# The second product of the last three chunks by Strassen's scheme: linear attention and a squared-ReLU layer on one core

## The chip, the cores and the metric

One core of one Trainium2 chip (trn2). The number that counts is the device time of one launch in microseconds. Before the change three runs took 1060.15, 1060.94 and 1062.51 us; the median is 1060.94.

## What is computed

Eight batches of eight heads, 576 tokens, head size 64. A linear attention gives each token 512 numbers, and a two-layer network follows; everything is float32 in and out.

```
phi(x) = [exp(p), exp(-p)],  p = x @ w_phi - max|x @ w_phi|        # 64 -> 2 x 128
num = phi(q) @ (phi(k).T @ v);  den = phi(q) @ sum(phi(k)) + 1e-6
x   = num / den                                                    # 4608 tokens x 512
out = relu(x @ w_in) ** 2 @ w_out                                  # 512 -> 2048 -> 512
```

## The kernel before, in words

The work comes in two streams that share the engines. The attention goes through 32 pairs of heads (four pairs to a batch): the first six pairs by `early` (L661), the others by `visit` (L842) and `late` (L905). What a pair yields goes into a ring buffer of tokens as two float16 halves (`tokens`, L805), scaled by a power of two that `batch_scale` (L548) finds for each batch from the largest sum of |v|.

The layer takes the 4608 tokens in 18 chunks of 256, and each chunk in 8 blocks of 256 hidden units: 144 blocks, written by `moe(c, f)` (L994), numbered n = 8c + f. A block has a **first product** on TensorE (L1012), 24 matmuls of 256 columns: w_in and x are each held as a high and a low float16 half, and three of the four half products are summed. ScalarE takes the relu out of PSUM (L1021), squares it into `gh` (float32r, L1023) and once more into the PSUM bank (L1025); VectorE subtracts the two into a bfloat16 remainder `gl` (L305, called at L1028). Then the **second product** (L1040), 12 matmuls of 512 columns: low w_out with the upper half of `gh`, high w_out with `gh`, near w_out with `gl`, for two groups of 128 tokens and two groups of 128 hidden units. It adds up over the 8 blocks of a chunk in two PSUM banks `po`, which VectorE scales into `o` (L1058) and SP's queue stores (L1069). The first product has two PSUM buffers `ph`; one comes free when VectorE has made `gl`. `gh` and `gl` have three buffers each.

Once per launch w_in and w_out are read, rounded and split on VectorE, ScalarE and GpSimd (L420 to L540). They go to homes in SBUF that stay until the end: `win`, and `wh` and `wl` for w_out.

The order of all this is fixed when the program is built. Every step is added to a planner (`Plan`, L78) with its engine, what it waits for, the buffers it uses and a rank; `order` (L150) plays the plan through, giving each engine the ready step of least rank, and each engine's instructions are written in that order. Steps with ranks between -50 and `MOVED` (70.0, L51) don't keep the rank of the code: `improve` (L141) takes it from a table of numbers, `RANKS`, 1107 of them.

Of the kernel before, what the change touches and what calls it, by code (L numbers as in the profile page):

```python
# [35 lines left out]
NCH = NT // T  # L36
RING = 6 * T
# [13 lines left out]
MOVED = 70.0  # L51
# [26 lines left out]
class Plan:  # L78
# [71 lines left out]
    def order(self):  # L150
# [20 lines left out]
        def release(op):  # L171
            least = max([open_at.get(tag, 0.0) for tag, n in alone(op)] + [a.start + 0.001 for a in op.behind], default=0.0)
# [74 lines left out]
class Tiles:  # L247
# [44 lines left out]
def tile_kernel(ctx, tc, qp, kp, vp, w_phi, w_in, w_out, out):  # L292
# [64 lines left out]
    vm_ = tiles(sm, "vm", [128, NP], F32, 2)  # L357
# [12 lines left out]
    o_ = tiles(mp, "o", [128, DM], F32, 2)  # L370

# [176 lines left out]
    def batch_scale(b, rank):  # L548
        last = []
        for i in range(NP):  # L550
# [3 lines left out]
                accum_out=vm_[b][:, i:i + 1]), [v_load[p]], [("v", p), ("vm", b), ("sx", ("va", p))], rank))  # L554
        d = cb[:, b, :]

        o = power(lambda: m1[b], d, TOP_X, [P.add("DVE", 0.2, lambda: V.tensor_reduce(
            out=m1[b], in_=vm_[b], op=ALU.max, axis=AX.X), last, [("vm", b)], rank)], [], rank)
        t0, t1 = b * S, (b + 1) * S
# [13 lines left out]
        scale_of[b] = P.add("DVE", 0.33, tokens, [o], [], rank)  # L573
# [234 lines left out]
    def tokens(p, nums, rank):  # L808
# [11 lines left out]
        for c0, c1 in cuts:  # L820
# [8 lines left out]
            def high(to=to, c0=c0, c1=c1):  # L829
                A.activation(out=to(0), in_=rb_[p][:, c0:c1], func=AF.Copy, scale=cb[:, b, 1:2])  # L830

            def low(to=to, c0=c0, c1=c1):
                V.scalar_tensor_tensor(out=to(1), in0=rb_[p][:, c0:c1], scalar=cb[:, b, 1:2], in1=to(0),
# [4 lines left out]
                    out=to(0), in0=rb_[p][:, c0:c1], scalar1=cb[:, b, 1:2], scalar2=None, op0=ALU.mult), 4.0))  # L838
# [155 lines left out]
    def moe(c, f, w_done):  # L994
# [9 lines left out]

        def gemm1():
# [11 lines left out]
        if f:  # L1017
            g1.after.append(chunk_done[c][-1])
        chunk_done.setdefault(c, []).append(g1)
        Q = m - 1000.0  # L1020
        o = P.add("ACT", act_us(512, 1), lambda: A.activation(  # L1021
# [6 lines left out]
        o = P.add("DVE", 0.70, lambda: sub(V, gl_[n], ph_[bank], gh_[n].bitcast(F32)),  # L1028
                  [o, sq], [("ph", bank), ("gh", n), ("gl", n)], Q)


        def gemm2():
# [5 lines left out]
            for s, i, j in turns:  # L1038
                g, w = ((gh_[n], highs[f]), (upper(gh_[n]), low), (gl_[n], near))[s]
                PE.matmul(out=po_[po[i][1]], lhsT=g[:, j, 128 * i:128 * i + 128], rhs=w[:, j, :],  # L1040
                          start=(f == 0 and (s, j) == (1, 0)), stop=(f == NFP - 1 and (s, j) == (2, 1)))

        g2 = P.add("PE", 2.74, gemm2, [o] + list(w_done[f, False]),
                   [("gh", n), ("gl", n)] + po, m + 1.5)
        if f:
            g2.after.append(last2[0])
        last2[0] = g2
        if f == NFP - 1:
# [3 lines left out]
    def store(c, i, po, g2, Q):  # L1052
        tt = 2 * c + i

        def scaled(E, x):
            to, of, k = o_[tt][:, x], po_[po[1]][:, x], cc[:, tt:tt + 1]
            if E is V:
                V.tensor_scalar(out=to, in0=of, scalar1=k, scalar2=k, op0=ALU.mult, op1=ALU.mult)  # L1058
            else:
                A.activation(out=to, in_=of, func=AF.Copy, scale=cc2[:, i:i + 1])  # L1060

        ways = ((V, slice(0, DM)),)
        if c == NCH - 1:
            ways = (V, slice(0, DM // 2)), (A, slice(DM // 2, DM))
        for E, x in ways:
            n = x.stop - x.start
            o = P.add(*(("DVE", dve_us(n) + 0.11) if E is V else ("ACT", out_us(n) + 0.09)), lambda E=E, x=x: scaled(E, x),
                      [g2] + [scales] * (E is A), [po, ("o", tt)], Q)
            P.add("SP", 0.38, lambda x=x: SP.dma_start(out[128 * tt:128 * tt + 128, x], o_[tt][:, x]), [o], [("o", tt)], Q,  # L1069
                  land=1.8, xfer=0.7)  # L1070
# [9 lines left out]
    def make_ring1():  # L1080
        stage.close()
        whole = ctx.enter_context(tc.tile_pool(name="late", bufs=1, side="right")).tile(
            [128, 2, KT, HR], F16, name="ring1")
# [21 lines left out]
    for p in range(NPAIR):  # L1105
        if p % NP == 0 and p:
# [3 lines left out]
            batch_scale(b, PER_PAIR * p + 1.0)  # L1110
# [3 lines left out]
        if p == EARLY:  # L1114
# [4 lines left out]
    cc2 = sm.tile([128, 2], F32, name="cc2")  # L1119
    last_cc = cc[:, 2 * NCH - 2:2 * NCH]  # L1120
    scales = P.add("DVE", 0.2, lambda: V.tensor_tensor(out=cc2, in0=last_cc, in1=last_cc, op=ALU.mult),
                   [scale_of[B - 1]], [], PER_PAIR * NPAIR, lock=4.0)
    for c in range(NCH):
        for f in range(NFP):
            moe(c, f, w_done)
    pool_next.after += pool_prep
    for op in P.ops:
        op.after = [x for a in op.after for x in (chunk_done[a[1]] if isinstance(a, tuple) else [a])]
# [65 lines left out]
```

## Time and profile before

| | us |
|---|---|
| median of three runs | 1060.94 |
| the profiled execution | 1060.65 |
| its span, first to last instruction | 1058.9 |
| TensorE busy | 1029.8 |
| VectorE busy | 744.2 |
| ScalarE busy | 632.3 |
| GpSimd busy | 135.6 |

The profiled execution is a run of its own: 1.75 us of its time lie outside the span. In the rows PE is TensorE's matmul, PEld its weight load, DVE VectorE, ACT ScalarE, POOL GpSimd, SP the engine that issues the DMAs. A group's row has the line of the code, the engine, the operation, output<-input by the program's names, the shapes, the count, and then busy time in us with the mean of one in ns; behind it stands the engine's idle time ahead of these instructions and what ended it. A matmul's duration includes its way through the array, so steps are read from start to start.

### The profile page before, as it was taken

What the parts mean: (1) busy time and instruction counts of PE and PEld (TensorE: products, weight loads), DVE (VectorE), ACT (ScalarE), POOL (GpSimd) and SP (SyncE); (2) the same over time, 40 slices, a digit from 0 to 9 for tenths busy, and PEclk for the clock granted to TensorE, in tenths of its full rate; (3) what the DMA queues carried; (4) which work ended last, traced back from release to release, by engine and by line L of the source; (5) the groups of instructions that cost most, each with busy time, mean ns of one, the idle gap of its engine ahead of it and who ended that gap; (6) DMA issues with size and microseconds to landing.
All of it is one profiled execution on the core that took longest, in us unless ns stands there. A gap on an engine that the chain in (4) does not pass through costs nothing.

```text
span 1058.9 us, 19521 instructions
## 1 busy us (share of the span) xinstructions
PE 1029.8 (97%) x7762; PEld 713.3 (67%) x7762; DVE 744.2 (70%) x1549; ACT 632.3 (60%) x1130; POOL 135.6 (13%) x66
## 2 busy tenths in 40 slices
PE   7887999999999999999999999999999999999998
PEld 5555666767676676666666667666766767677775
DVE  5899987987977868989878777877686775111111
ACT  5988875656667556755666655666565565333333
POOL 0011223011122001111111111111110111000000
PEclk9999999999999999999999999999999999999999
DMA  9634421221312211212222221112120101000000
GB/s 357 242 122 139 153 75 50 64 71 30 90 52 89 57 54 57 81 53 69 65 57 77 57 67 36 53 56 77 44 65 22 48 9 50 1 21 20 1 21 20
DMA packets 66143, 73.47 MB, mean 69 GB/s; under 512 B 35204, under 2 KB 44036, under 8 KB 64004
## 3 DMA queue, kind: packets, MB, share of 16 engines
q1 hardware_dynamic: 66052, 72.22, 21.8%
q8 instruction: 61, 1.00, 0.4%
q14 instruction: 30, 0.25, 0.1%
HBM read 59.18 MB, written 12.99 MB: 68 GB/s over the span
## 4 chain that ended last, share of the span: by engine, by line
PE 87%; DVE 7%; DMA 4%; ACT 1%; issue 1%; SPq 0%; DVEq 0%; ACTq 0%
PE po L1040 35%; PE ph L1012 34%; PE pv L645 5%; PE pn L863 3%; PE pp L589 2%; PE pv L863 2%; PE pp L933 2%; DMA rd<-rc 1%; PE pn L933 1%; PE pv L650 1%; DMA rb<-rd 1%; PE pn L595 1%; DVE u L466 1%; DVE rb L811 1%; DVE km L605 1%
## 5 line engine op out<-in xcount | busy, mean ns | idle before, releaser
L1012 PE MATMUL ph<-ring,win 128*128 128x256 f16 x3456 | 399.9, 273 | 1.4 <-DVE win L535 0.9
L1012 PEld LDWEIGHTS <-win 128*128 128x128 f16 x3456 | 336.3, 98 | 72.2 <-issue 8.7
L1021 ACT ACTIVATE r<-ph,cw 128x512 f32<-128x512 f32 x144 | 98.8, 686 | 227.1 <-PE ph L1012 226.6
L305 DVE TENSOR_TENSOR gl<-ph,gh 128x512 bf16<-128x512 f32 x144 | 98.5, 684 | 170.4 <-ACT ph L1025 169.0
L946 POOL PARTITION_ALL_REDUCE mx<-pt x52 | 113.6, 2184 | 615.5 <-ACT pt L309 441.6
L1040 PE MATMUL po<-wh,gh 128*128 128x512 f32 x576 | 184.2, 441 | 0.0
L1040 PE MATMUL po<-wl,gh 128*128 128x512 bf16 x576 | 148.6, 380 | 1.5 <-ACT gh L1023 1.4
L1040 PE MATMUL po<-wl,gl 128*128 128x512 bf16 x576 | 149.5, 382 | 0.0
L1040 PEld LDWEIGHTS po<-wh,gh 128*128 128x128 f32 x576 | 108.7, 189 | 33.0
L1023 ACT ACTIVATE gh<-r 128x512 fp32r<-128x512 f32 x144 | 91.0, 632 | 6.1 <-PE po L1040 1.5
L1040 PEld LDWEIGHTS <-gl 128*128 128x128 bf16 x576 | 44.7, 98 | 73.6 <-issue 31.7
L1040 PEld LDWEIGHTS <-gh 128*128 128x128 bf16 x576 | 53.4, 98 | 54.4 <-issue 11.4
L1025 ACT ACTIVATE ph<-r 128x512 f32<-128x512 f32 x144 | 83.9, 583 | 0.0
L645 PE MATMUL pv<-e,v 128*64 128x256 f32 x512 | 64.1, 392 | 3.0 <-ACT kz L309 1.4
L309 ACT ACTIVATE n<-pn 128x320 f32<-128x320 f32 (+1 forms) x32 | 13.8, 430 | 82.0 <-PE pn L863 81.1
L960 DVE SCALAR_TENSOR_TENSOR pt<-qe,zc,pt 128x576 f32<-128x576 f32 x52 | 42.4, 816 | 26.5 <-ACT pt L958 26.0
L305 DVE TENSOR_TENSOR qe<-pt,mx 128x576 f32<-128x576 f32 x52 | 39.1, 753 | 18.0 <-POOL mx L946 17.4
L611 ACT ACTIVATE e<-e 128x512 f32<-128x512 f32 x64 | 39.7, 621 | 19.5 <-DVE e L608 19.3
L645 PEld LDWEIGHTS pv<-e,v 128*64 128x64 f32 x512 | 36.7, 142 | 20.3 <-issue 3.2
L951 ACT ACTIVATE qe<-qe 128x576 f32<-128x576 f32 x52 | 35.0, 673 | 22.4 <-DVE qe L305 22.4
L958 ACT ACTIVATE pt<-qe,zc 128x576 f32<-128x576 f32 x52 | 40.2, 774 | 4.3
L964 DVE STREAM_TRANSPOSE yt<-pt 128x576 f32<-128x576 f32 x52 | 40.4, 776 | 1.5
(203 smaller groups left out, 1265.6 us busy)
## 6 DMA issues: line engine op xcount, KB each, us to landing
v<-in_vp_dram SPq DMA_DIRECT2D x32, 320.0 KB
k<-in_kp_dram SPq DMA_DIRECT2D x32, 288.0 KB
q<-in_qp_dram SPq DMA_DIRECT2D x32, 288.0 KB
rb<-rd SPq DMA_DIRECT2D x64, 144.0 KB
out_dram<-o SPq DMA_DIRECT2D x34, 256.0 KB
td<-kvs SPq DMA_DIRECT2D x26, 128.0 KB
kz<-td SPq DMA_DIRECT2D x104, 32.0 KB
raw3i<-in_w_in_dram SPq DMA_DIRECT2D x1, 1024.0 KB
```

Source lines behind the costliest of these rows:

```text
L305: eng.tensor_tensor(out=out_, in0=a, in1=b_, op=ALU.subtract)
L645: PE.matmul(out=to[64 * h:64 * h + 64, 0:256], lhsT=v_[p][:, t, h, :], rhs=e_[2 * p + h][:, t].rearrange("p s f -> p (s f)"), start=t == 0 ...
L863: PE.matmul(out=to[64 * h:64 * h + 64, :], lhsT=kz_[n][:, 128 * s_ + 64 * h:128 * s_ + 64 * h + 64], rhs=qe_[2 * n + h].rearrange("p (s x) ...
L946: o = P.add("POOL", par_us(S), lambda n=n, h=h: G.partition_all_reduce(mx_[n], pt_[p][:, h, :], channels=128, reduce_op=bass_isa.ReduceOp. ...
L958: o = P.add("ACT", act_us(S, 1), lambda h=h, qe=qe, y=y: A.activation(out=y(), in_=qe(0), func=AF.Copy, scale=zc_[p][:, 2 * h:2 * h + 1]), ...
L960: o = P.add("DVE", dve_us(S), lambda h=h, qe=qe, y=y: V.scalar_tensor_tensor(out=y(), in0=qe(1), scalar=zc_[p][:, 2 * h + 1:2 * h + 2], in ...
L964: o = P.add("DVE", dve_us(S), lambda n=n, y=y: V.transpose(yt_["y", n - 2 * EARLY], y()), [o], [("pt", p), ("yt", ("y", n - 2 * EARLY))], ...
L1012: PE.matmul(out=ph[:, j, :], lhsT=win[w][:, t, 128 * ff:128 * ff + 128], rhs=ring[half][x][:, t, c0:c0 + T], start=k == 0, stop=k == 3 * K ...
L1021: o = P.add("ACT", act_us(512, 1), lambda: A.activation(out=r_[n], in_=ph_[bank], func=AF.Relu, scale=cw[:, f, 0:1]), [g1], [("ph", bank), ...
L1023: sq = P.add("ACT", act_us(512), lambda: A.activation(out=gh_[n], in_=r_[n], func=AF.Square), [o], [("r", n), ("gh", n)], Q)
L1025: o = P.add("ACT", 0.59, lambda: A.activation(out=ph_[bank], in_=r_[n], func=AF.Square), [o], [("ph", bank), ("r", n)], Q, other=("DVE", 0 ...
L1040: PE.matmul(out=po_[po[i][1]], lhsT=g[:, j, 128 * i:128 * i + 128], rhs=w[:, j, :], start=(f == 0 and (s, j) == (1, 0)), stop=(f == NFP - ...
```

## The change

From chunk 15 on (`C0`), but for the very last block of chunk 17, a block's second product is done by Strassen's scheme. The 256 x 256 block of g (two token groups, two hidden groups) and the 256 x 512 block of w_out (two hidden groups, two output halves) are each cut in four; seven sums of the quarters are formed on either side, and seven products take the place of eight. Each is three matmuls of 256 columns in float16 (high with high, high with low, low with high), and each adds up over a chunk in half a PSUM bank of its own, in banks that the attention has left (`bank`). At the end of a chunk `gather` forms the four quarters of the output. This needs the following:

- `split_out`: for each of the 8 hidden blocks w_out is put together again from `wh` and `wl`, three groups of sums are formed, and the seven pieces split into float16 halves `sw`, most of them written over `wh` and `wl` once chunk 14 has read these.
- `norm`, `split_norms`, `tail_scale`: scales that keep the float16 in range, from norms of w_in's columns and of a chunk's tokens (ScalarE square, VectorE reduce, GpSimd all-reduce, a row of tiny VectorE steps).
- `batch_scale`: batches 6 and 7 share one scale, so v of batch 7 is also loaded, ahead of time, into one buffer `j`, and its |v| summed there.
- `RANKS`: 2432 numbers where there were 1107, for all steps with ranks up to 250, the whole program.

The core of the diff:

```
-MOVED = 70.0
+MOVED = 250.0
+C0 = 15
+LASTB = C0 * T // S
...
+    def split_block(c, f, n, ph, g1, m, Q):
...
+        o = P.add("ACT", act_us(512, 1), lambda: A.activation(
+            out=r_[n], in_=ph_[ph], func=AF.Relu, scale=cw_[c][:, f:f + 1]), [g1, norm_x[c]], ...
+        for t in range(2):
+            sq.append(P.add("ACT", act_us(256), lambda t=t: A.activation(
+                out=g()[:, 3 * t:3 * t + 6:5], in_=r_[n][:, :, 128 * t:128 * t + 128], func=AF.Square), ...
+        ss = [P.add("DVE", dve_us(256), ... ALU.add), ...
+              P.add("DVE", dve_us(256), ... ALU.subtract), ...
+              P.add("DVE", dve_us(128), ... ALU.add), ...]
+        o = P.add("ACT", act_us(896), lambda: A.activation(out=gh(), in_=g()[:, 1:8], func=AF.Copy), ss, ...
+        o = P.add("DVE", dve_us(896), lambda: sub(V, gl(), g()[:, 1:8], gh()), [o], ...
...
+        def products(some):
+            for i in some:
...
+                for k, (l, r) in enumerate(((gh, w["hi"]), (gh, w["lo"]), (gl, w["hi"]))):
+                    PE.matmul(out=to, lhsT=l()[:, a], rhs=r(slice(b_, b_ + 1))[:, 0], ...
...
+    def split_out(f, rank):
...
+        def whole():
+            V.tensor_tensor(out=flat_w()..., in0=highs[f]..., in1=wout[f][1]..., op=ALU.add)
...
+        for (at_, n), sm_, src, us_ in zip(WPART, sums, srcs, use):      # 512, 512, 512 and 256 columns
+            o = whole_op
+            if sm_:
+                o = P.add("DVE", dve_us(256 * n), sm_, ...
+            o = P.add("ACT", out_us(256 * n) + 0.09, lambda x=x, src=src: A.activation(
+                out=hi(x), in_=src(), func=AF.Copy, scale=wts[:, 3:4]), ...
+            o = P.add("DVE", dve_us(256 * n), lambda x=x, src=src: V.scalar_tensor_tensor(
+                out=lo(x), in0=src(), scalar=wts[:, 3:4], in1=hi(x), op0=ALU.mult, op1=ALU.subtract), ...
...
+    def gather(c, g2, kx, x_at, ky, y_at, Q):
+        first = [P.add("ACT", out_us(512) + 0.09, lambda j=j: A.activation(
+            out=a()[:, 2 * j:2 * j + 2], in_=x_at(j), func=AF.Copy, scale=ks()), ...) for j in range(2)]
+        o1 = P.add("DVE", dve_us(512), lambda: V.tensor_tensor(... first ...)
+        o = P.add("DVE", dve_us(512), lambda: V.tensor_tensor(... first ...)
+        o = P.add("DVE", dve_us(512), lambda: V.scalar_tensor_tensor(... [o, g2[1]] ...)
+        o2 = P.add("DVE", dve_us(512), lambda: V.scalar_tensor_tensor(... [o, g2[2]] ...)
...
     def store(c, i, po, g2, Q):
...
+        for x in (slice(0, 256), slice(256, 512)):
...
+            o = P.add("DVE", dve_us(256), lambda x=x, to=to: V.scalar_tensor_tensor(
+                out=to(), in0=po_[po[1]][:, x], scalar=cc2[:, 0:1], in1=to(), op0=ALU.mult, op1=ALU.add), ...
```

How the order moves, at three places. **TensorE, inside a second product**, before: the last of the low halves, the four with `wh`, the first with the remainder; po are the output banks, wh and wl parts of w_out.

```order
L1040 LDWEIGHTS gh_11442
L1040 MATMUL po_11429<-wl_642,gh_11442 128x512
L1040 MATMUL po_11426<-wh_631,gh_11442 128x512 x2
L1040 MATMUL po_11429<-wh_631,gh_11442 128x512 x2
L1040 LDWEIGHTS gl_11445
L1040 MATMUL po_11426<-wl_642,gl_11445 128x512
```

And now, one of the seven products (sw holds the split sums of w_out, its high half first, then its low half; v is the buffer in which the remainder lies):

```order
L1315 LDWEIGHTS gh_11035
L1315 MATMUL po_10983<-sw_10663,gh_11035 128x256
L1315 LDWEIGHTS gh_11035
L1315 MATMUL po_10983<-sw_10663,gh_11035 128x256
L1315 LDWEIGHTS v_11040
L1315 MATMUL po_10983<-sw_10663,v_11040 128x256
```

Twelve matmuls of 512 columns have become 21 of 256: seven of these groups of three.

**VectorE where chunk 14 ends** and the next begins, before: the remainders gl, and o, the two stores' tiles of a chunk.

```order
L305 TENSOR_TENSOR gl_10629<-ph_10587,gh_10626 128x512
L305 TENSOR_TENSOR gl_10673<-ph_10631,gh_10670 128x512
L1058 TENSOR_SCALAR o_10700<-po_10303,cc 128x512
L1058 TENSOR_SCALAR o_10702<-po_10306,cc 128x512
L305 TENSOR_TENSOR gl_10725<-ph_10675,gh_10722 128x512
```

And now, from one of the split steps up to the first remainder of a Strassen block (v_10972); L1204, L1216 and L1232 are `split_out`, qe holds a block's sums:

```order
L1232 SCALAR_TENSOR_TENSOR sw_10818<-e_10758,wts,sw_10818 128x512
L1093 TENSOR_SCALAR o_10863<-po_10439,cc 128x512
L1093 TENSOR_SCALAR o_10865<-po_10442,cc 128x512
L1216 TENSOR_TENSOR q_10868<-e_10758 128x512
L1232 SCALAR_TENSOR_TENSOR sw_10818<-k_10801,wts,sw_10818 128x512
L1204 TENSOR_TENSOR e_10898<-wh_1653,wl_1729 128x2x2x256
L1232 SCALAR_TENSOR_TENSOR sw_10818<-q_10868,wts,sw_10818 128x512
L1297 TENSOR_TENSOR qe_10902<-qe_10902 128x256 x2
L1297 TENSOR_TENSOR qe_10902<-qe_10902 128x128
L1216 TENSOR_TENSOR q_10938<-e_10898 128x512
L1297 TENSOR_TENSOR qe_10935<-qe_10935 128x256 x2
L310 TENSOR_TENSOR v_10972<-qe_10902,gh_10941 128x896
```

Where one subtraction followed another, with the stores between, the split of w_out now stands in the queue, its last hidden blocks ahead of and among the first Strassen blocks.

**TensorE at a pair's q projection** (L933, now L959), before: it stands between a first and a second product.

```order
L1012 LDWEIGHTS win_77
L1012 MATMUL ph_10144<-ring_0_78,win_77 128x256
L933 MATMUL pp_10176<-q_9576,wraw 128x288 x2
L933 MATMUL pn_10179<-q_9576,wraw 128x288
L933 MATMUL pv_10181<-q_9576,wraw 128x288
L1040 LDWEIGHTS gh_10101
L1040 MATMUL po_9701<-wl_1728,gh_10101 128x512
```

And now, with a first product on both sides, the second of two in a row ahead of it:

```order
L1044 LDWEIGHTS win_77
L1044 MATMUL ph_10150<-ring_0_78,win_77 128x256
L959 MATMUL pp_10192<-q_9541,wraw 128x288 x2
L959 MATMUL pn_10195<-q_9541,wraw 128x288
L959 MATMUL pv_10197<-q_9541,wraw 128x288
L1044 LDWEIGHTS win_76
L1044 MATMUL ph_10205<-ring_0_78,win_76 128x256
```

Over the whole program, first and second products came mostly in turn before; now two or three first products and two to four second ones often follow each other. Up to about the thirtieth block TensorE's order of blocks and attention steps is the same but for a few swaps. In chunks 15 to 17 first products run ahead: ten of them (two of chunk 16) are out before the first Strassen block of chunk 15 is complete, and the other seven of the chunk follow it without a break.

More of the change, by code (lines that the diff above doesn't have):

```diff
@@ L171, in release @@
         def release(op):
-            least = max([open_at.get(tag, 0.0) for tag, n in alone(op)] + [a.start + 0.001 for a in op.behind], default=0.0)
+            least = max([open_at.get(tag, 0.0) for tag, n in alone(op) if n[0] != "m" or holder.get(tag) != n] + [a.start + 0.001 for a in op.behind], default=0.0)
             for eng in op.ways:
@@ L258, in __getitem__, with at @@
     def __getitem__(self, n):
+        return self.at(n)
+    def at(self, n, shape=None, dtype=None):
         if n not in self.made:
@@ L548, in batch_scale @@
     def batch_scale(b, rank):
-        last = []
+        last, use = [], [("vm", b)]
         for i in range(NP):
@@ L571, in tokens, with vm_n @@
                 copy(cc[0:64, c1:c1 + 1], d[0:64, 0:1])
-        scale_of[b] = P.add("DVE", 0.33, tokens, [o], [], rank)
+        o = P.add("DVE", 0.33, tokens, [o], [], rank)
+        for x in range(b, e):
+            scale_of[x] = o
+    def vm_n(b):
+        return NPAIR - b * NP if b == LASTB else NP
+    home_b = lambda b: min(b, LASTB)
     m1 = [cp.tile([128, 1], F32, name=f"m1_{b}") for b in range(B)]
@@ L1003, in moe @@
                 after += [o for t0, t1, o in ring_of[p] if t0 < c * T + T and t1 > c * T]
+        last = n == NCH * NFP - 1
+        split = c >= C0 and not last
+        gi = min(n, C0 * NFP)
+        if f == 0 and split:
+            tail_scale(c, after)
         def gemm1():
@@ L1020, in moe @@
         Q = m - 1000.0
+        if split:
+            split_block(c, f, n, bank, g1, m, Q)
+            return
         o = P.add("ACT", act_us(512, 1), lambda: A.activation(
@@ L1027, in moe @@
                       out=ph_[bank], in0=ph_[bank], scalar=cw[:, f, 0:1], in1=r_[n], op0=ALU.mult, op1=ALU.mult), None))
-        o = P.add("DVE", 0.70, lambda: sub(V, gl_[n], ph_[bank], gh_[n].bitcast(F32)),
-                  [o, sq], [("ph", bank), ("gh", n), ("gl", n)], Q)
+        o = P.add("DVE", 0.70, lambda: sub(V, gl_[gi], ph_[bank], gh_[n].bitcast(F32)),
+                  [o, sq], [("ph", bank), ("gh", n), ("gl", gi)], Q)
         def gemm2():
@@ L1053, in store, with scaled @@
         tt = 2 * c + i
[L1055 to L1062, printed above, removed]
-        if c == NCH - 1:
[L1064 to L1070, printed above, removed]
+        def scaled():
+            k = cc[:, tt:tt + 1]
+            V.tensor_scalar(out=o_[tt], in0=po_[po[1]], scalar1=k, scalar2=k, op0=ALU.mult, op1=ALU.mult)
@@ L1081, in make_ring1 @@
         stage.close()
-        whole = ctx.enter_context(tc.tile_pool(name="late", bufs=1, side="right")).tile(
-            [128, 2, KT, HR], F16, name="ring1")
+        late = ctx.enter_context(tc.tile_pool(name="late", bufs=1, side="right"))
+        whole = late.tile([128, 2, KT, HR], F16, name="ring1")
+        for x in (j_, n1_, n2_):
+            x.pool = late
         ring[1] = [whole[:, i] for i in range(2)]
@@ L1118, in tile_kernel @@
     visit(NPAIR)
[L1119 to L1122, printed above, removed]
+    square_of.after.append(scale_of[B - 1])
+    split_norms(PER_PAIR * 24.0 + 3.0)
     for c in range(NCH):
+        if c == C0:
+            for f in range(NFP):
+                split_out(f, LEAD + (C0 - 1) * NFP + f)
         for f in range(NFP):
@@ L1126, in tile_kernel, with late_of @@
     pool_next.after += pool_prep
+    def late_of(a):
+        if a[0] == "chunk":
+            return chunk_done[a[1]]
+        return [g2_of[(C0 - 1) * NFP + a[1]], split_w[a[1]]["whole"]]
     for op in P.ops:
-        op.after = [x for a in op.after for x in (chunk_done[a[1]] if isinstance(a, tuple) else [a])]
+        op.after = [x for a in op.after for x in (late_of(a) if isinstance(a, tuple) else [a])]
     P.close()
```

321 lines of the change are left out of this document (286 added, 35 removed).

## The prediction

> **What bounds the kernel now.** I read the page's busy times first, then the stretches.
>
> ```profile
> span 1058.9 us, 19521 instructions
> PE 1029.8 (97%) x7762; PEld 713.3 (67%) x7762; DVE 744.2 (70%) x1549; ACT 632.3 (60%) x1130; POOL 135.6 (13%) x66
> ```
>
> ```profile
> core 0: us, PE busy (x) PEld busy (x) DVE busy (x) ACT busy (x) POOL busy (x), PEclk, DMA share, GB/s
> 0.00:200.00 200.00, 174.61 (x1584) 119.38 (x1586) 171.70 (x299) 155.80 (x267) 30.81 (x18) 0.99 0.44 154
> 200.00:830.00 630.00, 630.00 (x4637) 435.55 (x4634) 497.62 (x1109) 384.59 (x707) 96.04 (x44) 1.00 0.21 60
> 830.00:895.00 65.00, 65.00 (x468) 44.90 (x467) 46.31 (x98) 36.07 (x64) 8.71 (x4) 1.00 0.12 35
> 895.00:1055.00 160.00, 160.00 (x1081) 113.49 (x1079) 28.02 (x44) 55.42 (x93) 0.00 (x0) 1.00 0.04 13
> ```
>
> TensorE idles 25.4 us in the first 200 and then not at all until 1055; its clock is full. Whatever shortens TensorE's work after 200 us comes off the time, if TensorE is still fed. In the last 160 us, where the changed chunks lie, VectorE works 28 us and ScalarE 55. TensorE's own waits show how well it is fed:
>
> ```profile
> PE po L1040 <- ACT gh L1023: 1.4, 1, 1.4
> PE ph L1012 <- DVE gl L305: 0.4, 2, 0.3
> ```
>
> These columns are the total, the count and the longest. The timeline of one block late in the program gives the unit of all that follows:
>
> ```profile
> 1036.44 2.78 PE L1012 MATMUL ph<-ring,win 128*128 128x256 f16 x24
> 1039.06 1.03 PE L1040 MATMUL po<-wl,gh 128*128 128x512 bf16 x4
> 1039.26 0.69 ACT L1021 ACTIVATE r<-ph,cw 128x512 f32<-128x512 f32 x1 [3.45 <-PE ph L1012]
> 1039.73 1.28 PE L1040 MATMUL po<-wh,gh 128*128 128x512 f32 x4
> 1039.98 0.63 ACT L1023 ACTIVATE gh<-r 128x512 fp32r<-128x512 f32 x1
> 1040.52 0.58 ACT L1025 ACTIVATE ph<-r 128x512 f32<-128x512 f32 x1
> 1040.85 1.04 PE L1040 MATMUL po<-wl,gl 128*128 128x512 bf16 x4
> 1041.13 0.69 DVE L305 TENSOR_TENSOR gl<-ph,gh 128x512 bf16<-128x512 f32 x1 [4.60 <-ACT ph L1025]
> 1041.73 0.49 PE L1012 MATMUL ph<-ring,win 128*128 128x256 f16 x3
> ```
>
> Start to start, a first product takes 1039.06 - 1036.44 = 2.62 us, 0.109 for each of its 24 matmuls; a second product takes 2.67, 0.222 for each of its 12. The chain from a first product to its remainder is 0.69 + 0.63 + 0.58 + 0.69 = 2.59 us.
>
> **The products.** A Strassen block has 21 matmuls of 256 columns in float16 with a new weight load ahead of each, the first product's form, whose loads hide:
>
> ```profile
> L1012 PEld LDWEIGHTS <-win 128*128 128x128 f16 x3456 | 336.3, 98 | 72.2 <-issue 8.7
> ```
>
> 98 ns of load lie beside 109 of matmul, so I take 21 x 0.109 = 2.29 us. Against 2.67 that saves 0.38 us in each of 23 blocks: **-8.7 us**. [...]
>
> Merging the scales of batches 6 and 7 drops one of eight such gathers on TensorE, two matmuls of this row, some **-0.3**:
>
> ```profile
> L396 PE MATMUL pn<-ident,m 128*128 128x128 f32 x16 | 3.2, 281 | 0.0
> ```
>
> **The work for the other engines.** Durations for the new steps come from these rows.
>
> ```profile
> L960 DVE SCALAR_TENSOR_TENSOR pt<-qe,zc,pt 128x576 f32<-128x576 f32 x52 | 42.4, 816 | 26.5 <-ACT pt L958 26.0
> L305 DVE TENSOR_TENSOR qe<-pt,mx 128x576 f32<-128x576 f32 x52 | 39.1, 753 | 18.0 <-POOL mx L946 17.4 <-PE pv L863 0.2
> L811 DVE TENSOR_TENSOR rb<-n,rb 128x576 f32<-128x576 f32 x32 | 27.9, 873 | 2.9 <-DMA rb<-rd 2.7
> L632 DVE TENSOR_TENSOR es<-ez 128x256 f32<-128x256 f32 x52 | 22.5, 432 | 1.3
> L618 DVE TENSOR_TENSOR et<-pn,kmt 128x128 f32<-128x128 f32 x32 | 8.8, 274 | 0.0
> L1058 DVE TENSOR_SCALAR o<-po,cc 128x512 f32<-128x512 f32 x34 | 25.9, 802 | 1.0 <-PE po L1040 0.9
> L403 DVE TENSOR_SCALAR pw<-pw 128x1 int32<-128x1 int32 x8 | 1.2, 154 | 0.3
> L1023 ACT ACTIVATE gh<-r 128x512 fp32r<-128x512 f32 x144 | 91.0, 632 | 6.1 <-PE po L1040 1.5
> L621 ACT ACTIVATE et<-et 128x128 f32<-128x128 f32 x32 | 9.6, 300 | 3.1 <-DVE et L618 3.0
> L830 ACT ACTIVATE ring<-rb,cb 128x576 f16<-128x576 f32 x15 | 11.6, 771 | 2.6 <-DVE rb L811 2.6
> ```
>
> Straight lines through them give, for VectorE, a sum of 512 columns 0.69, of 256 0.43, of 128 0.27, of 896 1.10, of 1024 1.24; a step with a scalar 0.06 more. For ScalarE, 256 columns cost 0.41 and 896 0.96.
>
> *A Strassen block.* ScalarE: relu 0.69, two squares 0.82, copy 0.96, together 2.47 us (before 1.90). VectorE: sums 0.43 + 0.43 + 0.27 and the remainder 1.10, together 2.23 (before 0.69). TensorE's 2.62 + 2.29 = 4.91 cover both. The chain is 4.7 us instead of 2.59, but first products run ahead and `ph` is now free after the relu alone. Where Strassen products run without a break, the copy for the fourth waits until the first is done with its `gh`; 0.96 + 1.10 us follow while two products of 2.29 run. VectorE's 2.23 stays 0.06 below 2.29, so a run of seven just holds. I take 0.
>
> *The split of w_out.* For each hidden block VectorE has 1.24, then sums of 0.69 + 0.69 + 0.43, then remainders of three times 0.75 and one of 0.49: 5.8 us, 46 in all; ScalarE has 2.6, 21 in all. It can start only when the attention is nearly over and must be done, block by block, before chunk 15 reads it. I followed the queues at its densest place. From the remainder of chunk 14's third block to that of its last, VectorE has 12 steps with a scalar and 11 without of 512 columns, four of 1024, seven of 256, four of 576 and nine tiny ones: 9.0 + 7.6 + 5.0 + 3.3 + 3.1 + 1.4 = 29.4 us. TensorE meanwhile has five second products, five first ones and the attention's last step, which takes 901.50 - 899.41 = 2.1 us:
>
> ```profile
> 899.41 1.30 PE L863 MATMUL pn<-qe,kz 128*64 128x320 f32 x8
> ...
> 901.50 1.04 PE L1040 MATMUL po<-wl,gh 128*128 128x512 bf16 x4
> ```
>
> That is 28.6 us, and VectorE starts 5.34 - 2.59 = 2.75 ahead (two second products stand between a first product and its remainder's use). 2.0 us are left. From there to the first Strassen remainder VectorE has three steps of 0.69, six of 0.75, one of 1.24, the maximum of the token norms 0.43, eight tiny steps 1.2, two stores 1.6, five sums 2.0 and the remainder itself 1.10: 14.1 us, against one second and four first products, 13.2. So 1.1 us is left of 43.5. Behind that the two engines are ahead, since six more first products and the whole chunk's second ones follow. The cover is thin: **+0.7**, with bounds 0 and 5.9 (in L811's row this shape takes 873 ns on the mean, in L305's 753: 16% more, for 43.5 us 7.0, less the 1.1).
>
> *Norms and the early load of v.* Some 11 reductions of 1.24 us on VectorE with squares on ScalarE and as many all-reduces on GpSimd, mostly in the stretch from 200 to 830, where VectorE is busy 498 of 630 us and GpSimd 96; and four loads of v on SP's queue, moved ahead of some of the attention's loads, where the DMA engines are at 0.21 of their time. Hidden: 0. Uncovered, the eight reductions of w_in alone would be 10 us.
>
> **The new order in the middle.** With first products two in a row, a third one that follows after only a q projection must find its `ph` bank freed 3.8 us after the first of them ended (2.62 and a projection of 1.17), while the chain of 2.59 shares its queues with the attention:
>
> ```profile
> 760.60 0.76 PE L933 MATMUL pp<-q,wraw 64*128 64x288 f32 x4
> ...
> 761.77 1.04 PE L1040 MATMUL po<-wl,gh 128*128 128x512 bf16 x4
> ```
>
> Before, two places had this, and the waits' row says what they cost, 0.4 us together; now I count seven. Five more at 0.2: **+1.0**, bounds 0 and 1.5 (longest 0.3 each).
>
> **The end.** Now:
>
> ```profile
> 1054.56 0.60 PE L1040 MATMUL po<-wl,gl 128*128 128x512 bf16 x2
> 1055.20 0.54 DVE L1058 TENSOR_SCALAR o<-po,cc 128x256 f32<-128x256 f32 x1 [0.80 <-PE po L1040]
> 1055.78 0.47 ACT L1060 ACTIVATE o<-po,cc 128x256 f32<-128x256 f32 x1 [0.87 <-DVE o L1058]
> ```
>
> The last result is ready at 1056.25, 1.1 us after TensorE's end at 1055.16. After the change, four of the seven sums of chunk 17 are done 9 x 0.109 + 2.67 = 3.65 us before TensorE's end. Then ScalarE copies twice (2 x 0.69), VectorE takes four steps (0.69 + 0.69 + 0.75 + 0.75) and four of 256 columns (0.49 each): 6.2 us, 2.6 behind TensorE's end. **+1.5**, bounds 1 and 2.5.
>
> **The sum.** -8.7 - 0.3 + 0.7 + 1.0 + 1.5 = -5.8. Against the profiled execution 1060.65 - 5.8 = 1054.9; the median of the runs is 0.3 higher, so **1055.2 us**. The start is taken as unchanged: TensorE's order there differs by a few swaps.
>
> **Rivals.**
>
> 1. *VectorE becomes the bound from chunk 13 to 15 and the time rises.* TensorE would stand at the first Strassen product, or ahead of it at chunk 14's remainders. For it: 1.1 us left of 43.5, and steps that share their time with other engines take longer. Against: the steps were reckoned with loaded rows, and behind them the queues get ahead. The gain is used up when TensorE waits 5.8 us more than forecast, 6.5 in all, so when these 43.5 us run (6.5 + 1.1) / 43.5 = 17% longer than reckoned. At 30% VectorE is 13.0 us late, TensorE waits 11.9, and the time is 1055.2 - 0.7 + 11.9 = 1066. 0.11 for this rival, most of it on the slower side.
> 2. *The order in the middle stalls more.* Four second products now follow their own first product by only 3.1 to 3.8 us. If each waits the 1.4 us of the waits' row, that is 5.6 more: 1060.8. Against: before, two places of 3.8 us and less show no wait. 0.08.
> 3. *The new list moves the start.* 25.4 us of TensorE's idle time are open to it in the first 200. A fifth of it gained is 5 us: 1050; as much can be lost: 1060. 0.12 gained, 0.06 lost.
> 4. *The Strassen products don't step at 109 ns,* as three matmuls to a sum and then another bank are no form of this trace. If every load showed, a block's product would take 21 x (98 + 109) ns = 4.35 us, 2.06 more than forecast: 1055.2 + 47 = 1102. The break-even is 2.67 / 21 = 0.127 us per matmul, before the other terms. Against it stand 3456 matmuls of this form that step at 109. 0.03. [...]
>
> That leaves 0.60 for the forecast, 1051.5 to 1058.5 with its bounds. About 0.2% (2 us) is what a measurement of this kernel can tell from no change. Faster by more than that needs a time under 1058.8: the forecast, the gained start, and a part of the first two rivals and of the lost start, 0.79. Slower by more, over 1063.1: most of the first rival, the fourth and a little of the others, 0.11. Between: 0.10. The range takes in the gained start and, above, the first two rivals' middle prices: 1049.5 to 1060.5.
>
> **What the profile of the changed kernel would show.** Right: 21 matmuls in 2.29 us between starts, 4.91 us for a block on average in chunks 15 to 17; TensorE idle less than 2 us between 200 us and its end; VectorE ending some 2.6 us after TensorE; the idle time of the first 200 us within 2 us of 25.4. Wrong: waits of TensorE on VectorE at the first Strassen product (rival 1) or spread over 200 to 830 us (rival 2), another idle sum at the start (rival 3), a step above 0.12 us (rival 4).

## The result, and the profile after

The changed kernel takes **1055.66 us** (median of six runs, 1053.69 to 1058.27); the kernel before, beside it on the same chip, 1061.20 (six runs, 1058.99 to 1062.91). The ratio is 0.995 with a 95% interval of 0.9931 to 0.9968: 5.5 us faster. The forecast was 1055.2. How it comes about is another matter: some terms of the sum were right, others were wrong and offset each other by luck.

The profiled execution took 1056.05 us. Its page:

```profile
span 1054.3 us, 20229 instructions
PE 1021.2 (97%) x7967; PEld 726.7 (69%) x7967; DVE 852.9 (81%) x1748; ACT 682.6 (65%) x1211; POOL 158.6 (15%) x78
```

And its stretches, with the columns of the prediction's (busy us of PE, PEld, DVE, ACT and POOL, granted clock, DMA share, GB/s):

```profile
0.00:200.00 200.00, 174.07 (x1578) 119.08 (x1578) 172.34 (x301) 156.48 (x267) 31.39 (x18) 0.97 0.45 154
200.00:830.00 630.00, 628.36 (x4641) 435.01 (x4639) 513.28 (x1121) 396.97 (x723) 111.71 (x53) 1.00 0.21 62
830.00:895.00 65.00, 65.00 (x459) 44.50 (x457) 54.38 (x112) 38.86 (x69) 10.08 (x4) 1.00 0.14 38
895.00:1050.00 155.00, 153.73 (x1297) 128.14 (x1295) 111.62 (x214) 90.28 (x155) 5.38 (x3) 1.00 0.04 13
```

TensorE is busy 8.6 us less, VectorE 108.7 us more, and TensorE still sets the time. In the first 200 us it idles 25.9 us (25.4 before). New is the idle time of 630.0 - 628.36 = 1.64 us in the second stretch, where it had none. The waits of TensorE behind 200 us are two:

```profile
PE pp L959 <- DVE e L634: 1.6, 1, 1.6
PE po L1315 <- DVE v L310: 0.3, 1, 0.3
```

The timeline of a Strassen block in chunk 15: its first two matmuls, and the first of the next block.

```profile
970.49 0.27 PE L1315 MATMUL po<-pt,gh 128*128 128x256 f16 x1
970.60 0.27 PE L1315 MATMUL po<-ez,gh 128*128 128x256 f16 x1
...
972.78 0.27 PE L1315 MATMUL po<-n,gh 128*128 128x256 f16 x1
```

From 970.49 to 972.78 are 2.29 us for 21 matmuls, 0.109 each, as forecast. The groups of the new steps:

```profile
L310 DVE TENSOR_TENSOR v<-qe,gh 128x896 f16<-128x896 f32 x23 | 24.9, 1087 | 24.1 <-ACT gh L1303 24.1
L1303 ACT ACTIVATE gh<-qe 128x896 f16<-128x896 f32 x23 | 21.7, 944 | 15.2 <-PE po L1315 9.2 <-PE pv L1315 4.3 <-PE pp L1315 1.6
L1127 DVE TENSOR_REDUCE n<-j 128x256 f32<-128x1024 bf16 x11 | 21.5, 1952 | 3.5 <-POOL n L1129 2.4 <-ACT qe L977 0.8 <-ACT j L1126 0.3
```

The remainder of 896 columns (1087 ns, reckoned 1.10 us) and its copy (944 ns, reckoned 0.96) came out as reckoned. The norm reductions did not: 1952 ns each, where the prediction had 1.24 us. The timeline around the 1.6 us wait shows one of them:

```profile
700.83 1.94 DVE L1127 TENSOR_REDUCE n<-j 128x256 f32<-128x1024 bf16 x1
...
710.05 0.41 DVE L1140 TENSOR_REDUCE wn<-n 128x1 f32<-128x256 f32 x1
...
710.50 0.27 DVE L1141 TENSOR_SCALAR wn<-wn,cw 128x1 f32<-128x1 f32 x1
...
710.81 0.16 DVE L1147 TENSOR_REDUCE wnm<-wn 128x1 f32<-128x8 f32 x1
710.89 0.68 DVE L634 TENSOR_TENSOR e<-pp,km 128x512 f32<-128x512 f32 x1
...
711.71 0.76 PE L959 MATMUL pp<-q,wraw 64*128 64x288 f32 x4 [1.64 <-DVE e L634]
```

The q projection needs the bank `pp`, which VectorE frees with `e`; ahead of `e` in VectorE's queue stand steps of `split_norms`. The other wait has the same company. VectorE and TensorE in chunk 15:

```profile
956.91 1.92 DVE L1127 TENSOR_REDUCE n<-j 128x256 f32<-128x1024 bf16 x1
960.82 1.94 DVE L1127 TENSOR_REDUCE n<-j 128x256 f32<-128x1024 bf16 x1 [1.99 <-POOL n L1129]
962.68 2.08 DVE L310 TENSOR_TENSOR v<-qe,gh 128x896 f16<-128x896 f32 x2
...
963.82 0.28 PE L1315 MATMUL po<-sw,v 128*128 128x256 f16 x1 [0.26 <-DVE v L310]
```

Two norm reductions with a wait for GpSimd between them hold VectorE for 5.8 us, and the remainders that TensorE needs stand behind them. The end, by VectorE's first gather step, TensorE's last matmuls and VectorE's last steps:

```profile
1046.65 0.69 DVE L1344 TENSOR_TENSOR e<-e 128x512 f32<-128x512 f32 x1 [3.65 <-ACT e L1342]
...
1048.38 0.61 PE L1075 MATMUL po<-wl,gl 128*128 128x512 bf16 x2
...
1049.57 1.65 DVE L1103 SCALAR_TENSOR_TENSOR e<-po,cc,e 128x256 f32<-128x256 f32 x4
```

TensorE ends at 1048.99 and the last result is ready at 1051.22, 2.23 us later (before 1.09).

### The profile page after: what moved, and what is told of

The parts are those of the page before. It is cut to its first block, busy times and chain, and to the rows that moved or that the text cites. A ratio compares the mean times of both kernels' runs of the same rounds, so it can differ in the third digit from the quotient of the medians.

```text
span 1054.3 us, 20229 instructions
## 1 busy us (share of the span) xinstructions
PE 1021.2 (97%) x7967; PEld 726.7 (69%) x7967; DVE 852.9 (81%) x1748; ACT 682.6 (65%) x1211; POOL 158.6 (15%) x78
## 4 chain that ended last, share of the span: by engine, by line
PE 84%; DVE 7%; DMA 4%; ACT 2%; issue 1%; SPq 0%; POOL 0%; ACTq 0%; DVEq 0%; POOLq 0%
PE ph L1044 34%; PE po L1075 29%; PE pv L671 4%; PE pp L615 3%; PE pn L889 3%; PE pv L889 2%; PE pp L959 2%; DMA raw1o<-in_w_out_dram 2%; PE po L1315 1%; PE pp L1315 1%; DMA den<-sx 1%; PE pn L959 1%; PE pv L676 1%; PE pn L621 1%; PE pn L1315 1%
## 5 line engine op out<-in xcount | busy, mean ns | idle before, releaser
L1056 ACT ACTIVATE r<-ph,cw 128x512 f32<-128x512 f32 x121 | 83.0, 686 | 119.9 <-PE ph L1044 119.2
L1075 PE MATMUL po<-wh,gh 128*128 128x512 f32 x484 | 155.0, 441 | 0.0
L1075 PE MATMUL po<-wl,gh 128*128 128x512 bf16 x484 | 124.8, 379 | 1.1 <-DVE o L1093 1.0
L1075 PE MATMUL po<-wl,gl 128*128 128x512 bf16 x484 | 125.7, 382 | 0.0
L310 DVE TENSOR_TENSOR gl<-ph,gh 128x512 bf16<-128x512 f32 x121 | 82.8, 684 | 50.9 <-ACT ph L1060 37.0
L1075 PEld LDWEIGHTS po<-wh,gh 128*128 128x128 f32 x484 | 91.4, 189 | 27.8
L1058 ACT ACTIVATE gh<-r 128x512 fp32r<-128x512 f32 x121 | 75.9, 627 | 11.3 <-PE po L1075 7.2
L1075 PEld LDWEIGHTS <-gh 128*128 128x128 bf16 x484 | 45.7, 98 | 50.3 <-issue 6.3
L1060 ACT ACTIVATE ph<-r 128x512 f32<-128x512 f32 x121 | 71.3, 589 | 1.3
L986 DVE SCALAR_TENSOR_TENSOR pt<-qe,zc,pt 128x576 f32<-128x576 f32 x52 | 42.2, 815 | 23.8 <-ACT pt L984 23.5
L314 ACT ACTIVATE n<-pn 128x320 f32<-128x320 f32 (+1 forms) x32 | 13.7, 429 | 52.9 <-PE pn L889 51.6
L310 DVE TENSOR_TENSOR v<-qe,gh 128x896 f16<-128x896 f32 x23 | 24.9, 1087 | 24.1 <-ACT gh L1303 24.1
```

The lines of the kernel that those rows point to most:

```text
L310: eng.tensor_tensor(out=out_, in0=a, in1=b_, op=ALU.subtract)
L986: o = P.add("DVE", dve_us(S), lambda h=h, qe=qe, y=y: V.scalar_tensor_tensor(out=y(), in0=qe(1), scalar=zc_[p][:, 2 * h + 1:2 * h + 2], in ...
L1056: o = P.add("ACT", act_us(512, 1), lambda: A.activation(out=r_[n], in_=ph_[bank], func=AF.Relu, scale=cw[:, f, 0:1]), [g1], [("ph", bank), ...
L1058: sq = P.add("ACT", act_us(512), lambda: A.activation(out=gh_[n], in_=r_[n], func=AF.Square), [o], [("r", n), ("gh", n)], Q)
L1060: o = P.add("ACT", 0.59, lambda: A.activation(out=ph_[bank], in_=r_[n], func=AF.Square), [o], [("ph", bank), ("r", n)], Q, other=("DVE", 0 ...
```

## The experiments

The theory after this reading: TensorE is the bound, the saving is a count of matmuls, and what was lost besides lies on VectorE, at the norm reductions, with a thin cover at the change-over from chunk 14 to 15. The rivals: the new order of the steps loses or wins the time; or another engine paces the last chunks.

**Three matmuls more in each Strassen block.**

```
-                for k, (l, r) in enumerate(((gh, w["hi"]), (gh, w["lo"]), (gl, w["hi"]))):
+                three = ((gh, w["hi"]), (gh, w["lo"]), (gl, w["hi"]))
+                for k, (l, r) in enumerate(three * 2 if i == 7 else three):
```

> The third product of each Strassen block's last group is added twice: 24 matmuls of 256 columns instead of 21 (one of the seven sums is so counted double; nothing else changes, nor does the order). 24 x 0.109 = 2.62 us is within 0.05 us of the 2.67 that the plain second product took, so this takes the saving on TensorE back and leaves everything else of the change in place. Theory A, TensorE is the bound and the saving is a count of matmuls: 23 x 3 x 0.109 = 7.5 us more than the changed kernel, 1055.7 + 7.5 = 1063.2, some 2 us above the kernel before. Rival B, in the last three chunks another engine sets the pace and TensorE waits in hidden places: the three matmuls fit into those waits, less than 3 us more, under 1059.

Measured: 1062.91 us, ratio to before 1.0018 (1.0008 to 1.0029). Against the changed kernel that is 7.25 us for 69 matmuls, 0.105 each. In the tail TensorE has no idle time to hide them in:

```profile
895.00:1035.00 140.00, 140.00 (x1190) 117.66 (x1189) 103.65 (x201) 83.27 (x145) 5.38 (x3) 1.00 0.04 15
```

Theory A holds. With the saving on TensorE nearly taken back, the rest of the change costs some 2 us over the kernel before.

**A third of the second product left out.**

```
-                for k, (l, r) in enumerate(((gh, w["hi"]), (gh, w["lo"]), (gl, w["hi"]))):
+                for k, (l, r) in enumerate(((gh, w["hi"]), (gl, w["hi"]))):
```

> The low half of w_out is left out of the products: 14 matmuls a Strassen block instead of 21 (a third of the second product is not computed). Theory A, TensorE stays the bound throughout the last three chunks: 23 x 7 x 0.109 = 17.5 us less than the changed kernel, 1038.2, no waits of TensorE on the remainders. Theory B, VectorE's 2.23 us a block become the pace where seven Strassen products stand in a row (14 x 0.109 = 1.53 us each now): about five blocks of each of three rows lose 2.23 - 1.53 = 0.7 us, 10.5 in all at most, so 1044 to 1049, and the profile shows waits of TensorE on the remainder step (v) in those rows.

Measured: 1042.33 us, ratio 0.9831 (0.9816 to 0.9845), 13.3 us less than the changed kernel and between the two theories. One wait of TensorE on VectorE is longer:

```profile
964.82 0.28 PE L1315 MATMUL po<-sw,v 128*128 128x256 f16 x1 [2.20 <-DVE v L310]
```

And a stretch behind it has half the clock:

```profile
966.00:968.00 2.00, 2.00 (x11) 1.45 (x10) 2.00 (x6) 1.86 (x4) 0.00 (x0) 0.50 0.03 8
```

This wait is 1.9 us longer than the 0.3 of the changed kernel, the slow matmuls behind it cost 1.7 (some 16 steps of 0.21 us in place of 0.109), and the wait at the q projection is 0.7 longer (2.3 instead of 1.6): 17.5 - 4.3 = 13.2. Theory B's pace is not it: there is a single wait, none in the other rows of Strassen products, and it stands at the pair of norm reductions shown above. VectorE's 2.23 us a block are hidden even when TensorE's are 1.53; the norms are not.

**Half of each norm reduction.**

```
-            out=n1_[i], in_=box().rearrange("p k t -> p t k"), op=ALU.add, axis=AX.X), ...
+            out=n1_[i], in_=box()[:, 0:2].rearrange("p k t -> p t k"), op=ALU.add, axis=AX.X), ...
```

> The eleven reductions of squared norms on VectorE add two of the four slices (half of the sum is left out), so each has 512 elements instead of 1024 and should take some 1.0 us instead of 1.94; the order of the work is the same. Theory A, the only wait of TensorE between 200 and 830 us (1.6 us, a q projection that stands for VectorE's e at 711 us) comes from these reductions, which had been taken to be hidden: the wait goes, and so does most of the 0.3 us ahead of a Strassen remainder at 964; 1055.7 - 1.9 = 1053.8. Rival B, the new order of the middle makes the wait: it stays within 0.3 us of 1.6, and the time within 0.5 of 1055.7 but for the spread of the runs.

Measured: 1052.33 us, ratio 0.9919 (0.9906 to 0.9933). Behind 200 us no wait of TensorE is left. The row of the reductions:

```profile
L1127 DVE TENSOR_REDUCE n<-j 128x256 f32<-128x512 bf16 x11 | 7.4, 677 | 2.8 <-POOL n L1129 2.0 <-ACT j L1126 0.8
```

And the stretch that had the 1.6 us:

```profile
630.00:830.00 200.00, 200.00 (x1495) 140.27 (x1492) 160.45 (x355) 135.20 (x239) 45.43 (x23) 1.00 0.18 53
```

Both waits are gone: theory A, and the order in the middle is acquitted. The time fell by 3.3 us where 1.9 were expected; in this profile the first 200 us idle 23.5 us instead of 25.9, with the same instructions in the same order there.

**The remainders of the split of w_out done twice.**

```
-            o = P.add("DVE", dve_us(256 * n), lambda x=x, src=src: V.scalar_tensor_tensor(
-                out=lo(x), in0=src(), ..., op1=ALU.subtract),
+            o = P.add("DVE", dve_us(256 * n), lambda x=x, src=src: [V.scalar_tensor_tensor(
+                out=lo(x), in0=src(), ..., op1=ALU.subtract) for _ in range(2)],
```

> Each remainder step of the split of w_out is done twice, with the same result: 32 more steps on VectorE, 21.9 us, of which 18 of 512 columns and 4 of 256 stand ahead of the first Strassen remainder, 18 x 0.67 + 4 x 0.4 = 13.7 us by their distance in the changed kernel's profile. Theory A, the cover at the change-over is thin (1.1 us reckoned; in the changed kernel's profile VectorE idles 0.6 us in this stretch and the first remainder ends 1.9 us ahead of its use): TensorE comes to stand ahead of or at the first Strassen product for 13.7 - 0.6 - 1.9 = 11 us, 1055.7 + 11 = 1067, with less than 2 us more behind it. Rival B, the remainders of chunk 14 and of the first Strassen blocks have more slack than that, as first products run ahead: TensorE waits under 5 us, under 1061.

Measured: 1078.15 us, ratio 1.0162 (1.0148 to 1.0177): 22.5 us more than the changed kernel. TensorE's waits behind 830 us:

```profile
PE ph L1044 <- ACT r L1288: 6.1, 1, 6.1
PE ph L1044 <- DVE gl L310: 3.1, 1, 3.1
PE po L1075 <- DVE gl L310: 2.9, 2, 1.7
PE po L1315 <- DVE v L310: 2.4, 1, 2.4
PE po L1315 <- ACT gh L1303: 2.3, 1, 2.3
```

The longest of them in the timeline:

```profile
948.40 7.93 PE L1044 MATMUL ph<-ring,win 128*128 128x256 f16 x48 [6.15 <-ACT r L1288]
```

TensorE's clock (the number ahead of the last two) in two stretches behind it:

```profile
948.00:950.00 2.00, 1.60 (x8) 1.13 (x8) 2.00 (x3) 1.94 (x5) 0.00 (x0) 0.50 0.06 15
...
954.00:956.00 2.00, 2.00 (x21) 1.80 (x19) 1.44 (x4) 1.97 (x5) 0.00 (x0) 1.00 0.00 0
```

Ahead of the first Strassen product TensorE waits 6.1 + 3.1 + 2.9 = 12.1 us, for 13.7 added: nearly the 11 of theory A. Its time of 1067 was missed by 11 us all the same, since two costs had been left out. Behind it come 4.7 us more, at the place of the norm pair. And after the long waits the clock is at half: the 48 matmuls of the last timeline row take 7.93 us instead of 5.40, 2.5 more, and some 16 Strassen matmuls later 1.7 more. 12.1 + 4.7 + 2.5 + 1.7 = 21.0, of a span that grew by 22.1; the wait at the q projection (2.5 instead of 1.6) is most of the rest.

The 6.15 us show how a wait travels. TensorE stands for a `ph` that ScalarE's relu frees, and the relu was ready. It stands in ScalarE's queue behind a copy of a split piece (L1229), which waited 7.6 us for VectorE's sum. In the changed kernel the same copy waits 4.4 us and nobody suffers.

**Only the last two of the four remainders twice.** Against the edit above:

```
-... op1=ALU.subtract) for _ in range(2)],
+... op1=ALU.subtract) for _ in range(1 + (x.start > 2))],
```

> Of the four remainder steps of the split of w_out only the last two are done twice, with the same result: ahead of the first Strassen remainder that is six steps of 0.67 and four of 0.4, 5.6 us more on VectorE, against 13.7 in the run that doubled all four. Theory A, there is a cover of one to two us at the change-over and each us beyond it is waited for by TensorE: waits of 5.6 - 1.6 = 4 us in all up to the first Strassen product, where 1.6 is what the run with all four left covered (13.7 against 12.1 us of waits), and at most 1 us behind it; no single wait above 3 us, so TensorE's clock stays at 1.00; 1055.7 + 4 = 1059.7. Rival B, the cover is larger and the doubled run fell over an edge (the scale of chunk 15 that came late and stopped first products): under 1.5 us of waits, 1057 or less.

Measured: 1066.36 us, ratio 1.0042 (1.0028 to 1.0056), 10.7 more than the changed kernel. The two long waits:

```profile
942.12 6.72 PE L1044 MATMUL ph<-ring,win 128*128 128x256 f16 x48 [4.34 <-ACT r L1288]
...
974.20 0.28 PE L1315 MATMUL po<-sw,v 128*128 128x256 f16 x1 [2.55 <-DVE v L310]
```

Ahead of the first Strassen product TensorE waits 4.34, and 0.26 at another place: 4.6 for 5.6 added. So the cover is 1.0 us here and 1.6 in the run above; 1.1 had been reckoned. The first number of the expectation was right and the time was not: a single wait did exceed 3 us and the clock fell (0.83 on the mean from 935 to 945 us; 6.72 - 5.40 = 1.3 us), the norm pair added 2.3 and its slow matmuls 1.7 (they step at 0.21 us behind a wait of 2.55; that the clock stays at 1.00 up to waits of 3 us, as the expectation has it, no run shows, and behind the 2.20 us in the run with 14 matmuls it was at 0.50), and the wait at the q projection grew from 1.6 to 3.0. What the expectation gave in brackets, the scale of chunk 15, was not the step that came late: it was the same copy on ScalarE.

**The norms reduced in two halves, whole.**

```
+        def summed():
+            V.tensor_tensor(out=box()[:, 0:2], in0=box()[:, 0:2], in1=box()[:, 2:4], op=ALU.add)
+            V.tensor_reduce(out=n1_[i], in_=box()[:, 0:2].rearrange("p k t -> p t k"), op=ALU.add, axis=AX.X)
```

> Each reduction of squared norms on VectorE is done in two steps: the two halves of the four slices are added in place (512 elements), then two slices are reduced (512 elements, 0.68 us in the run that left half of the sum out). The whole sum is computed again, order and number of planned steps as in the changed kernel. Theory A, what made TensorE wait at the q projection is VectorE's time for the reduction, 1.95 us a piece, well above the 1.24 reckoned: with 0.69 + 0.68 less an overlap of 0.1, some 1.3 us, the 1.6 us wait goes or falls under 0.5, and the time is that of the run with half the sum within its spread, 1052 to 1054.5. Rival B, only the halved run was short enough: at 1.3 us the wait stays above 1 us and the time is 1055 or more.

Measured: 1053.01 us, ratio 0.9925 (0.9912 to 0.9937), and no wait of TensorE on VectorE behind 200 us: theory A. The groups of the two steps:

```profile
L1129 DVE TENSOR_REDUCE n<-j 128x256 f32<-128x512 bf16 x11 | 7.6, 687 | 1.1 <-POOL n L1132 0.4
L1128 DVE TENSOR_TENSOR j<-j 128x512 bf16<-128x512 bf16 x11 | 5.7, 516 | 1.7 <-ACT j L1126 1.7
```

687 + 516 ns do what took 1952. The time by itself would not settle it, as the interval overlaps the changed kernel's 0.9931 to 0.9968; the wait that is gone does.

**One gather step at the end on GpSimd.**

```
-        o1 = P.add("DVE", dve_us(512), lambda: V.tensor_tensor(
+        o1 = P.add("DVE", dve_us(512), lambda: (G if c == NCH - 1 else V).tensor_tensor(
```

> In the gather of chunk 17 alone, the first of VectorE's four steps (the sum of two scaled products that only the last additions need) is done by GpSimd, which idles there. Theory A, the end is VectorE's chain and packed: it starts its second step 0.6 us sooner, and the last result follows TensorE's end by 2.23 - 0.6 = 1.6 us; GpSimd needs about half of the 2.77 us that 1024 columns cost it elsewhere, 1.4, and is done before the last additions: 1055.7 - 0.6 = 1055.1, to be read in the profile and not in the median. Rival B, VectorE's steps get longer while GpSimd works beside them, or the last additions wait for GpSimd: the result follows TensorE's end by 2.2 us or more as before.

Measured: 1055.25 us, ratio 0.9943 (0.993 to 0.9955), which is the changed kernel's within the spread. The profile decides: GpSimd's step, TensorE's last matmuls, VectorE's last steps.

```profile
1045.13 1.77 POOL L1344 TENSOR_TENSOR e<-e 128x512 f32<-128x512 f32 x1 [75.91 <-ACT e L1342]
...
1046.80 0.61 PE L1075 MATMUL po<-wl,gl 128*128 128x512 bf16 x2
...
1047.39 1.65 DVE L1103 SCALAR_TENSOR_TENSOR e<-po,cc,e 128x256 f32<-128x256 f32 x4
```

The last result is ready at 1049.04, 1.63 us behind TensorE's 1047.41, where it was 2.23: theory A. VectorE's steps take 0.69 and 0.75 us beside GpSimd's 1.77, where they took 0.68 and 0.75.

**Both kernels without their lists of ranks.** One line each, `P.improve()` becomes `P.order()`.

> The changed kernel with its list of ranks unused: the planner orders the work by the ranks that the code gives. To be read beside the kernel before with its list unused. Theory A, the gain is a property of the products and the new list only has to keep other engines out of the way: changed less before, both without lists, is -9.0 (products and scale gather) + 1.1 (end) + 0 to 6 for the norms and the split of w_out at unchosen places, so -8 to -2 us. Rival B, the new list carries the gain: without it the split of w_out comes in the way and the difference is above 0. Both kernels should be slower than with their lists.

> The kernel before with its list of ranks unused: the planner orders the work by the ranks that the code gives. It serves as the base for the changed kernel without its list. Theory A (the gain lies in the products): 2 to 8 us above the changed kernel without its list. Rival B (the gain lies in the new list): below it. How much the list itself is worth is not known from any row; some tens of us at most, as TensorE's idle time is 25 us with it.

Measured: 1060.00 us for the changed kernel (ratio 1.0000, 0.9987 to 1.0013) and 1064.35 for the one before (1.0038, 1.0021 to 1.0055). The difference is -4.35, inside theory A's -8 to -2, and the two intervals do not overlap: the gain does not hang on the new list. A list is worth 4.3 us to the changed kernel (1060.00 - 1055.66) and 3.6 to the one before (1064.35 - 1060.75, its runs on the same chip).

**Both edits together.**

> Both single edits together in the changed kernel: norm reductions in two halves, and the first step of chunk 17's gather on GpSimd. Theory A, the two are in different places and add up: the run with halves alone had 1053.0, the end gives 0.6 more, 1052.4, with the result 1.6 us behind TensorE's end and no wait of TensorE on VectorE between 200 and 830 us. Rival B, the gain of the halves was a lucky start: the wait is gone but the time is back at 1055 or more.

Measured: **1051.48 us**, ratio 0.9906 (0.9891 to 0.992), 9.7 us below the kernel before; the interval lies clear of the changed kernel's 0.9931 to 0.9968. TensorE has no wait behind 200 us, and its end and the last result are 1.65 us apart:

```profile
1043.70 0.60 PE L1075 MATMUL po<-wl,gl 128*128 128x512 bf16 x2
...
1044.30 1.65 DVE L1103 SCALAR_TENSOR_TENSOR e<-po,cc,e 128x256 f32<-128x256 f32 x4
```

This version beats both kernels.

## Why the prediction was right, and where it was wrong

| term | forecast | in the profile of after |
|---|---|---|
| products | -8.7 | -8.7 (483 steps of 0.109 us) |
| scale gather | -0.3 | two matmuls fewer, -0.4 |
| change-over | +0.7 | 0 |
| norms, early load of v | 0 | +1.9 (waits of 1.6 and 0.3) |
| order in the middle | +1.0 | 0 |
| the end | +1.5 | +1.1 |
| the start | 0 | +0.5 |

*Products:* right in size and reason. The step of 0.109 us carried over to three matmuls a sum with a new weight load each, and the run with 69 more matmuls gave the price back, at 0.105 us each.

*A Strassen block's cover, 0:* right. With the products cut by a third it still holds but for one place.

*Change-over, +0.7:* the cover was right in size, with 1.1 us reckoned and 1.0 to 1.6 found, and the change-over itself cost nothing, which lies within the bounds of 0 and 5.9. The 0.3 us that TensorE waits stand later, in chunk 15, and the runs with shorter norms remove them, so they are counted there. The first rival was rightly feared and its mechanism is real, but its price was too low: the extra work there costs more than its own time, through ScalarE's queue and the clock (13.7 us of it ahead of the first Strassen product came with 22.5 us more, 5.6 with 10.7). The rival's other premise, steps that take longer with another engine at work, shows in the kernel before at 75.33 us: the sum of L811 takes 2.70 us, with GpSimd at work from 74.56 to 77.41, where the median of its 32 is 0.75.

*Norms, "Hidden: 0":* **this step failed.** The prediction took a reduction of 1024 elements at 1.24 us from a straight line through additions, and took VectorE's mean load over 630 us for cover. A reduction took 1.95 us, and the eight for w_in stand within 62 us (the last starts at 700.83, and between 700 and 705 VectorE was busy 4.90 us of 5). So `e` came late. VectorE itself stood 0.94 us for ScalarE on the way (up to 707.85), so the delay does not run through VectorE's queue alone; that the reductions cause it is shown by the runs that shorten them. Shorter reductions take the wait away three times out of three, with the order unchanged; in the six profiles that keep both the list and the reductions (the changed kernel's among them) it is there each time, 1.6 to 3.0 us.

*Order in the middle, "+1.0":* **this step failed as well.** No first product waits for its `ph` in the middle. The chain of 2.59 us fits into 3.8 at all the new places. The price had been read at the wrong place: both waits of the row with 0.4 us stand in the first 200 us of the kernel before,

```profile
152.40 2.78 PE L1012 MATMUL ph<-ring,win 128*128 128x256 f16 x24 [0.28 <-DVE gl L305]
...
158.02 2.78 PE L1012 MATMUL ph<-ring,win 128*128 128x256 f16 x24 [0.17 <-DVE gl L305]
```

and behind 200 us TensorE had no wait at all, as its stretch with 630.00 us busy of 630.00 said. The 1.4 us of the second rival come from the same early part (at 167.48); that rival, of the same mechanism, is refuted too.

The 1.9 us missed at the norms and the 1.7 put in here and at the change-over that did not come nearly cancel. That the sum came out so close is luck.

*The end, +1.5:* right in mechanism, 1.1 in size. The copies took 0.63 us each where 0.69 was reckoned, and the last four steps 1.65 us together where four times 0.49 was; that VectorE's chain is the end was shown by taking one step out of it.

*The start, 0:* within what can be told. With one and the same list the idle time of the first 200 us was 25.9, 24.7, 26.4, 23.5 and 26.5 us in five profiles (the changed kernel and the first four experiments), 25.4 in the kernel before. This spread of 3 us is in every comparison here.

The right-hand column adds to -5.6, and the profiled span fell by 4.6. Of the difference 0.4 lies between the last result and the end of the program (3.05 us, before 2.63). Some 0.6 us of TensorE's time is not assigned; the clock of the first 200 us, 0.97 where it was 0.99, may hold part of it, which no run shows.

## What to carry to other kernels

Where a saturated engine gets shorter work of a form that its trace already shows, the saving can be counted in instructions and trusted (-8.7 us forecast here and found); look for the loss in the helpers. Price each helper by a row of its own form (here a reduction of 1024 elements took 1952 ns, an addition of as many 1216), and look for its cover in the few us where it stands, not in the mean load of a long stretch. A sum that comes out right is no proof of its terms: ask the trace for each wait by name.

## What the hardware showed besides

**After some waits TensorE ran at half its clock.** After the 6.15 us wait some 24 matmuls stepped at 0.213 us instead of 0.109, after the 4.34 us wait some 12, and after a wait of only 2.20 us some 16, with a granted clock of 0.50. There the slow steps began later than the first matmul: the first five still stepped at 0.11, and from 965.37 to 968.74 us they were slow. It doesn't follow from the length alone: at the q projection waits of 1.6 to 2.5 us left the clock at 1.00 and one of 3.0 did not (0.50 from 714 to 716 us), and in the run with all remainders doubled a wait of 3.1 us had no slow step behind it (1.00 from 924 to 930 us). What decides it, no run here shows.

**A reduction over four short rows was dear here.** 256 sums of four elements, 512 bytes apart, took 1952 ns; 256 sums of two took 677, and an addition of 1024 elements (L1204) 1216. Why four cost nearly three times two was not tried. An in-place addition of 512 elements in bfloat16 took 516 ns on the mean, where float32 ones of that size (L1344) take 0.69 us.
